# Five small moves in an attention and feed-forward kernel on one core: a bank for the ones, a load in halves, and squares, stores and a scale at later steps

## The chip, the cores and the metric

The kernel runs on one core of one Trainium2 chip. The metric is the device time of one execution in microseconds. Before the change the median of 3 runs is 811.76 us (811.22 to 811.85).

A core has five engines, each of which works through its own row of instructions in order: TensorE (PE, matrix products), VectorE (DVE), ScalarE (ACT), GpSimd (POOL) and SyncE (SP), which here issues nearly all DMA transfers. Engines wait for each other by semaphores.

## The reference

`x` is 2048 x 512 in float32. It is normalised, goes through windowed attention with 32 heads of 16 and, beside that, through a gated feed-forward net with 1792 inner columns. The result is `x + s * g`.

```python
xn = _layernorm(x, axis=-1)
# s: attention; idx = arange(S), W = 256, Dh = 16, H = 32
qkv = (xn @ wqkv) ...                       # q, k, v per head
scores = einsum("bhqd,bhkd->bhqk", q, k) * (Dh ** -0.5)
mask = (idx[:, None] - idx[None, :] >= 0) & (idx[:, None] - idx[None, :] < W)
p = softmax(where(mask, scores, -1e9))
s = (p @ v) @ wo
# g: feed-forward
h = silu(xn @ w1) * (xn @ w3)
g = silu(h @ w2)
return x + s * g
```

## The kernel before, in words

Tokens are worked on in four tiles `t` of 512 (`NT`), each of four blocks `b` of 128. Heads are in four groups `g` of eight, and a group's heads in two passes `p`. The 1792 inner columns are 14 blocks `f` of 128.

A float32 operand of a product is cut into two float16 numbers, hi and lo, and a product is three matmuls: hi·hi, lo·hi, hi·lo. Before a weight matrix is cut, the squares of its entries are summed per row (on ACT by `activation` with `accum_out`, L249, or on DVE, L251), the sums are cast (L261) and added over all rows by matmuls with a matrix of ones (`powers`, L280 or, in a corner of a bank of scores, L285); a short chain on DVE (L291 to L304) makes a power of two of them, with which ACT cuts the hi part (L333, or L342 and L343) and DVE (L334) or POOL (L345) the lo part.

PSUM, where PE writes, has three kinds of banks: two for plain products that take turns (`m0`, `m1`, by `bank()`), two for scores (`s`, by `scores_bank()`) and one for sums of attention (`po`). PE cannot write a bank before it has been read.

The order on PE is that of the program. The order on the other engines is made by the scheduler when the kernel is built. The program itself holds a clock of steps: `later(n, f)` puts `f` into a list that is due `n` steps on, and a step passes with each batch of scores and each piece of dense work. `beside_scores(n, f)` does the same for norms by matmuls in a corner of the scores' banks.

At the start PE is fed with ones (`keep_busy`), the first tile is normalised and transposed (`turn`, L493, with XH copied by ACT at L496 and XL made by DVE at L501), and groups 0 and 1 of queries and keys are projected (`project`, L597; evacuated by ACT at L614 and DVE at L618). Projected queries and keys are stored to DRAM (`dQ`, `dK`) and fetched in another layout by `fetch`. Then `spread` mixes batches of scores (maxima: PE L665, DVE L679; probabilities: PE L746, DVE L753, ACT L756; values: PE L774) with dense work (gate and up: PE L1036, ACT L1051, DVE L1055 and L1060; down: PE L1261; output: PE L1313).

For the first tile, the gate and up weights of two blocks are loaded (L868), and `measure(f)` sums their squares, one block per step when `apart` is 1, and lets the norm follow by `beside_scores(8, scale)`. `measure(6)` is called five steps late. The down weights' squares are L923. `wout` does the same for the output weights in units 6 and 7. `total` makes an output block; its store to DRAM (L1324) is due four steps after it, and its buffers (`slot`, from a pool of 54 that all blocks share) come free with the store.

Of the kernel before, what the change touches and what calls it, by code (L numbers as in the profile page):

```python
# [10 lines left out]
F32 = mybir.dt.float32  # L11
# [72 lines left out]
def tile_block(ctx: ExitStack, tc: tile.TileContext, x, wqkv, wo, w1, w3, w2, out):  # L84
# [59 lines left out]
    def later(n, f):  # L144
        made_so_far[0] += 1
        queue.append((now[0] + n, made_so_far[0], f))
# [16 lines left out]
    def bank(shape, dtype=F32):  # L163

        open_bank[0] = b = 1 - open_bank[0]
        return psm.tile(shape, dtype, name=f"m{b}", tag=f"m{b}", bufs=1)
# [15 lines left out]
    def beside_scores(n, f):  # L182

        later(n, lambda: besides.insert(0, f))
# [396 lines left out]
    def project(t, g, k, terms=(range(3),), scores_bank=False):  # L581


        cell = {}

        parts = ([[(c, i) for c in (2 * half, 2 * half + 1) for i in range(3)] for half in range(2)] if len(terms) == 1
                 else [[(c, i) for i in group for c in range(NC)] for group in terms])

        def part(n):
            assert turned[t] == 4  # L590
            w = WQ[t, g, k]
            xh, xl = X[t]
            if n == 0:
                cell["pp"] = pss.tile([P, 2, TW], F32, name="s")[:, 0, :] if scores_bank else bank([P, TW])
            for c, i in parts[n]:
                a, b = ((0, xh), (1, xh), (0, xl))[i]
                nc.tensor.matmul(cell["pp"], w[:, (a * NC + c) * P:(a * NC + c + 1) * P], b[:, c, :], start=(c, i) == parts[0][0],  # L597
                                 stop=(c, i) == parts[-1][-1])
            if n < len(parts) - 1:
                return  # L600
            if t == 0:
                def store():
                    with behind_load():
                        nc.sync.dma_start(dWQ[g, k], w)
                    give(w, after=8)
                later(45, store)
            else:
                give(w)
            pp = cell["pp"]
            both = take(F16)  # L610
            B = both.rearrange("p (a t) -> p a t", a=2)
            s = QS / (XS * WS)
            with urgent():
                nc.scalar.activation(B[:, 0, :], pp, AF.Copy, scale=s)  # L614

            def rest():
                with urgent():
                    lasts["emptied"] = nc.vector.scalar_tensor_tensor(B[:, 1, :], pp, s, B[:, 0, :], op0=ALU.mult, op1=ALU.subtract)  # L618
                d = (dQ, dK)[k][g][:, :, t * TW:(t + 1) * TW]
                if k == 0:  # L620
                    nc.sync.dma_start(d[:, 0:2, :], B[:, 0:1, :].to_broadcast([P, 2, TW]))
                    nc.sync.dma_start(d[:, 2, :], B[:, 1, :])
                else:
                    nc.sync.dma_start(d[:, 0:2, :], B)
                    nc.sync.dma_start(d[:, 2, :], B[:, 0, :])
                give(both, after=4)
            later(1, rest)
        return opening([(len(l), lambda n=n: part(n)) for n, l in enumerate(parts)])
# [2 lines left out]
        WQ[t, g, k] = w = take(F16)  # L631
        nc.sync.dma_start(w, dWQ[g, k])

    def fetch(t, g):
        QA[t, g] = qa = qpool.tile([P, 4, TW], F16, name="qa")
        ka = keys(t, g)
        c0 = 0 if t else 2 * P
        for dst, d in ((ka[:, :, c0:], dK[g][:, :, t * TW - 2 * P + c0:(t + 1) * TW]),
                       (qa, dQ[g][:, :, t * TW:(t + 1) * TW])):
            for r in range(2):  # L640
                lasts["load"] = nc.sync.dma_start(dst[64 * r:64 * r + KR],
                                  d[64 * r:64 * r + 64].rearrange("(a d) i t -> (d i) a t", d=DH))

# [224 lines left out]

    measured = set()

    def measure(f, apart=0):

        raws = [RAW.pop(f + i) for i in range(2)]
        sb = squares([raws[0][0], raws[1][0], raws[0][1], raws[1][1]], on_act=4 if f > 2 else 2, apart=apart)

        def scale(s=None):
            pp = small.tile([P, 2, 2], F32, name="pp")
            pi = small.tile([P, 2, 2], F32, name="pi")  # L880
            return then(s, powers(sb, 4, pp.rearrange("p a b -> p (a b)"), pi.rearrange("p a b -> p (a b)"), s),
                        lambda: rest(pp, pi))

        def rest(pp, pi):
            ff = slice(f, f + 2)
            nc.vector.tensor_scalar(sg_scale[:, ff], pp[:, 0, :], 0.5 / (WS * XS), None, op0=ALU.mult)
            nc.vector.tensor_mul(p13[:, ff], pp[:, 0, :], pp[:, 1, :])
            measured.update((f, f + 1))

            def cut(i, k):  # L890
                if k == 0:
                    WF[0, f + i] = [[None, None], WF.pop((0, f + i), [None, None])[1]]
                WF[0, f + i][0][k] = a = take(F16)
                split_pool(a[:, 0:D], a[:, D:], raws[i][k], pi[:, k, i:i + 1])
                give(raws[i][k], after=5)
            for i in range(2):
                for k in range(2):
                    later(((1, 2, 4, 6) if f < 8 else (1, 5, 9, 13))[2 * i + k], lambda i=i, k=k: cut(i, k))
        if started:
            beside_scores(8, scale)  # L900
        else:
            later(10 if apart else 6, scale)

# [389 lines left out]
    def total(t, b):  # L1293

        r = slice(t * TW + b * P, t * TW + (b + 1) * P)
        cell = {}

        def part(half):
            WOH, WOL = SQ["wo"][:2]
            tb = slice(b * P, (b + 1) * P)  # L1300
            if half == 0:
                cell["ps"] = bank([P, D])
                assert (t, b) in summed
                cell["y"] = y = take(F32)
                acc = ACC[t, b]
                with behind_exp():
                    nc.scalar.activation(y, acc, AF.Tanh, scale=0.5)
                nc.vector.scalar_tensor_tensor(y, y, 1.0, acc, op0=ALU.add, op1=ALU.mult)
                give(acc)
            ps, y = cell["ps"], cell["y"]  # L1310
            for g in (2 * half, 2 * half + 1):
                for i, (a, w) in enumerate(((0, WOH), (0, WOL), (1, WOH))):
                    nc.tensor.matmul(ps, O[t, g][:, a, tb], w[g], start=g == 0 and i == 0,  # L1313
                                     stop=g == NG - 1 and i == 2)
            if half:
                with urgent():
                    lasts["emptied"] = nc.vector.scalar_tensor_tensor(y, ps, sc["y"], y, op0=ALU.mult, op1=ALU.mult)
                if t == NT - 1:
                    nc.vector.tensor_add(y, y, XR[t, b])
                else:  # L1320
                    halves(nc.gpsimd.tensor_add, y, y, XR[t, b])

                def store():
                    nc.sync.dma_start(out[r, :], y)  # L1324
                    give(y, XR[t, b], after=30)
                if t == NT - 1:
                    store()
                else:
                    later(4, store)
                if b == 3:  # L1330
                    give(*(OT[t, g] for g in range(NG)))
        return opening([(6, lambda h=h: part(h)) for h in range(2)])
# [22 lines left out]
    def feed_forward():  # L1355
# [4 lines left out]
        for t in range(NT):  # L1360
            for f in range(FB):
                if t == 0:
# [3 lines left out]
                    elif f + LEAD == FB - 1:  # L1366
                        pieces += [(0, lambda f=f: load(0, f)) for f in range(FB - 2, FB)]
                    if f % 2 and f + 3 < FB:
                        pieces.append((0, lambda f=f + 3: later(5, lambda: measure(f, 1)) if f == 6 else measure(f, 1)))
                    pieces += [(0, lambda f=f: load_down(0, f)) for f in range(f + 2 if f else 0, min(f + 3, FB))]  # L1370
                    for m in range(f + 1 if f else 0, min(f + 2, FB)):
                        k = next(k for k, (_, f1) in enumerate(GROUPS) if m < f1)
# [158 lines left out]
        nc.gpsimd.memset(KA[2][:, a, :].bitcast(F32), TWO_ONES)  # L1531


    def keep_busy(n):
        ps = bank([P, 4, P])
        for _ in range(n):
            nc.tensor.matmul(ps, onesb, onesb.unsqueeze(1).to_broadcast([P, 4, P]), start=True, stop=True)

# [19 lines left out]
        flush()  # L1558
    with tc.issue_after(lasts["hi"].ins), tc.issue_after(lasts["x"].ins):
        qk[1][1]()  # L1560
    keep_busy(4)


    k00, q00 = (project(0, 0, k, ((0,), (1,), (2,)), k) for k in (1, 0))
    run([k00[0], q00[0], k00[1]])
    qk[1][2]()
    with tc.issue_after(lasts["scale"].ins):
# [2 lines left out]
    qk[1][3]()  # L1570
    with tc.issue_after(lasts["hi"].ins):
        run([k00[2], q00[2]])
    later(1, lambda: fetch(0, 0))
    k01 = project(0, 1, 1, ((0, 2), (1,)))
    run(k01[:1])
    wv[2]()
# [4 lines left out]
    sc["o"] = scaled(SQ["wv"][3], OS / WS, "so")  # L1581
    with tc.issue_after(lasts["hi"].ins):
        measure(0)
    run(project(0, 1, 0, scores_bank=True))
    later(1, lambda: fetch(0, 1))
    run(value(0, True))
    qk[2][1]()
# [35 lines left out]
    for n, u in enumerate(units):  # L1623
# [7 lines left out]
            wout[0]()  # L1631
        if n == 7:
            wout[1](2)
            beside_scores(12, lambda s: then(s, wout[2](s), lambda: later(2, lambda: wout[3](2)), lambda: later(3, out_scale)))
        want += a_unit - other[n]
        mine = more(want)

# [39 lines left out]
```

## Time and profile before

| | |
|---|---|
| median of 3 runs | 811.76 us |
| the profiled execution | 811.24 us |
| its span on the core | 809.4 us |
| PE busy | 793.7 us (98%) |
| DVE busy | 631.2 us (78%) |
| ACT busy | 392.1 us (48%) |
| POOL busy | 377.1 us (47%) |
| granted TensorE clock | 1.00 throughout |

Times in rows of the trace are in microseconds from the start of the span: first the start, then how long, then the engine and the line of the kernel, the operation, what is written from what and how large it is. In brackets stands how long the engine stood idle before the row and what ended it. "SPq" is SP's queue: how long the issue of a DMA took, not its transfer.

### The profile page before, as it was taken

Reading aid. Unit: us, or ns where it says so; the run is one execution under the profiler, and the core shown is the slowest. Engines: PE = TensorE matmul, PEld = TensorE weight load, DVE = VectorE, ACT = ScalarE, POOL = GpSimd, SP = SyncE. Lnnn points to the kernel's source line nnn. Section 1 sums busy time; section 2 is a strip of 40 time slices with the busy share of each in tenths; the row PEclk is TensorE's granted clock in tenths of the full one; section 3 lists DMA queues with packets and bytes.
Section 4 is the critical chain, followed back from the end, with each engine's and each line's share of the span. In section 5 each row is a group of like instructions: output and inputs, shape, how many; then the busy total and the mean of one; then the engine's idle time right before and its main releaser. Section 6 shows DMA issues by size and latency. Waiting matters only on the chain.

```text
span 809.4 us, 23944 instructions
## 1 busy us (share of the span) xinstructions
PE 793.7 (98%) x9176; PEld 403.7 (50%) x9176; DVE 631.2 (78%) x2037; ACT 392.1 (48%) x591; POOL 377.1 (47%) x732
## 2 busy tenths in 40 slices
PE   8999989999999999999999999999999999999998
PEld 4444444444444444444444454456544754466465
DVE  8788788887888777887988888777778787875437
ACT  6879586553546544345344433344444234344411
POOL 2345376342329445354353455530346276550670
PEclk9999999999999999999999999999999999999999
DMA  9968554835576474757655634646372644335321
GB/s 282 265 214 267 160 183 134 278 114 191 160 199 208 134 232 139 218 142 263 160 162 181 194 104 119 185 137 179 105 201 74 160 139 137 113 90 172 111 65 62
DMA packets 109795, 134.19 MB, mean 166 GB/s; under 512 B 18864, under 2 KB 64880, under 8 KB 109680
## 3 DMA queue, kind: packets, MB, share of 16 engines
q1 hardware_dynamic: 109392, 132.13, 54.6%
q8 instruction: 72, 1.18, 0.6%
q10 hardware_dynamic: 288, 0.52, 0.2%
q14 instruction: 43, 0.35, 0.1%
HBM read 91.23 MB, written 36.57 MB: 158 GB/s over the span
## 4 chain that ended last, share of the span: by engine, by line
PE 79%; DVE 8%; ACT 6%; DMA 3%; issue 2%; SPq 1%; POOL 0%; ACTq 0%; DVEq 0%
PE m L1036 30%; PE po L774 8%; PE m L1261 8%; PE m L1179 8%; PE m L597 7%; PE s L746 5%; PE m L1313 4%; PE m L567 4%; PE s L665 3%; DMA slot<-in_B_w_dram 2%; DVE junk L679 2%; PE po L665 2%; ACT slot L342 1%; ACT pt L756 1%; ACT sqa L249 1%
## 5 line engine op out<-in xcount | busy, mean ns | idle before, releaser
L1036 PE MATMUL m<-XH,slot 128*128 128x512 f16 x896 | 267.4, 380 | 1.6 <-DVE slot L618 1.2
L756 ACT ACTIVATE pt<-s,es 128x1024 f32<-128x1024 f32 x152 | 167.5, 1112 | 193.7 <-DVE s L753 186.5
L1036 PEld LDWEIGHTS <-slot 128*128 128x128 f16 x1344 | 124.7, 98 | 156.0 <-issue 12.0
L1036 PE MATMUL m<-XL,slot 128*128 128x512 f16 x448 | 169.9, 379 | 0.0
L753 DVE TENSOR_TENSOR s<-s,MK 128x256 f32<-128x256 f32 (+2 forms) x280 | 118.7, 434 | 51.2 <-PE s L746 47.0
L679 DVE CUSTOM_DVE_ANT_0 junk<-s,MW 128x320 bf16<-128x320 f32 x276 | 133.9, 485 | 17.9 <-PE s L665 10.3
L339 POOL TENSOR_TENSOR slot<-slot,slot 128x256 f16<-128x256 f32 (+1 forms) x86 | 57.7, 692 | 141.9 <-ACT slot L1069 76.7
L345 POOL TENSOR_TENSOR slot<-slot,slot 128x128 f16<-128x128 f32 x168 | 69.1, 446 | 58.3 <-ACT slot L343 58.3
L679 DVE CUSTOM_DVE_ANT_0 junk<-po,MW 128x320 bf16<-128x320 f32 x172 | 83.4, 485 | 4.7 <-DVE mt L704 0.3
L1261 PE MATMUL m<-slot,slot 128*128 128x512 f16 x336 | 78.6, 380 | 0.3 <-DVE slot L1055 0.3
L774 PE MATMUL po<-pt,V 64*32 64x320 f32 (+4 forms) x2880 | 77.2, 342 | 0.8 <-DVE pp L304 0.8
L597 PE MATMUL m<-XH,slot 128*128 128x512 f16 x240 | 71.0, 380 | 1.6 <-DVE slot L1055 1.2
L1179 PE MATMUL m<-slot,slot 128*128 128x256 f16 x588 | 68.4, 273 | 0.0
L1094 POOL TENSOR_TENSOR slot<-slot,slot 128x256 f16<-128x256 f32 x98 | 64.6, 671 | 1.1
L1051 ACT ACTIVATE slot<-m,sgs 128x512 f32<-128x512 f32 x56 | 38.3, 683 | 54.4 <-PE m L1036 52.3
L774 PEld LDWEIGHTS po<-pt,V 64*32 64x32 f32 x2880 | 50.5, 106 | 22.9 <-PE s L515 0.9
L1179 PEld LDWEIGHTS <-slot 128*128 128x128 f16 x588 | 56.1, 98 | 11.5 <-issue 3.0
L1055 DVE SCALAR_TENSOR_TENSOR slot<-slot,m 128x512 f32<-128x512 f32 x56 | 38.3, 684 | 29.0 <-ACT slot L1051 29.0
L746 PE MATMUL s<-qa,KA 50*64 50x320 f16 (+3 forms) x1472 | 58.4, 260 | 0.1
L597 PEld LDWEIGHTS <-slot 128*128 128x128 f16 x384 | 35.6, 98 | 44.8 <-issue 3.4
L746 PEld LDWEIGHTS <-KA 50*64 50x64 f16 x1472 | 30.1, 106 | 51.9 <-issue 30.9
L1261 PEld LDWEIGHTS <-slot 128*128 128x128 f16 x336 | 30.7, 98 | 38.6 <-issue 4.2
(189 smaller groups left out, 1138.5 us busy)
## 6 DMA issues: line engine op xcount, KB each, us to landing
slot<-dW SPq DMA_DIRECT2D x98, 256.0 KB
slot<-in_B_w_dram SPq DMA_DIRECT2D x56, 256.0 KB
slot<-dFold SPq DMA_DIRECT2D x48, 256.0 KB
dW<-slot SPq DMA_DIRECT2D x42, 256.0 KB
slot<-in_A_x_dram SPq DMA_DIRECT2D x30, 256.0 KB
KA<-dK SPq DMA_DIRECT2D x24, 288.0 KB
qa<-dQ SPq DMA_DIRECT2D x32, 192.0 KB
slot<-dWQ SPq DMA_DIRECT2D x24, 256.0 KB
```

The lines of the kernel that those rows point to most:

```text
L339: op(out[:, c], a[:, c], b[:, c])
L345: nc.gpsimd.tensor_sub(lo[:, c:c + P], raw[:, c:c + P], hi[:, c:c + P])
L597: nc.tensor.matmul(cell["pp"], w[:, (a * NC + c) * P:(a * NC + c + 1) * P], b[:, c, :], start=(c, i) == parts[0][0], stop=(c, i) == parts[ ...
L679: lasts["maximum"] = nc.vector.tensor_tensor_reduce(out=junk[:, :n], in0=s[:, r, :n], in1=mask, scale=1.0, scalar=NEG, op0=ALU.add, op1=AL ...
L746: nc.tensor.matmul(s[64 * h:64 * h + 64, r, o:o + 64 * n], ka[rows, 2 * p + a, 64 * (m + 4):64 * (m + 5)], qa[rows, 2 * p + a, 64 * (m + k ...
L753: nc.vector.tensor_add(v, v, MK[:, kind, of:of + n, :].unsqueeze(1).to_broadcast([P, 2 * len(which), n, 64]))
L756: lasts["exp"] = nc.scalar.activation(pt, s, AF.Exp, scale=es)
L774: nc.tensor.matmul(cell["po"][32 * i:32 * i + 32, h, 64 * (m + k):64 * (m + k + n)], V[64 * h:64 * h + 64, (4 * t + m // 2) % VB, hd * VW: ...
L1036: nc.tensor.matmul(cell[k], w[:, (a * NC + c) * P:(a * NC + c + 1) * P], b[:, c, :], start=c == 0 and i == 0, stop=c == NC - 1 and i == 2)
L1094: nc.gpsimd.tensor_sub(lo, view, hi)
L1179: nc.tensor.matmul(cell["ps"][:, c], made[:, f:f + P], wj[:, g:g + 256], start=j == j0 and c == 0 and n == 0, stop=j == j1 - 1 and n == 2, ...
L1261: nc.tensor.matmul(ps, hh[:, a * TW + b * P:a * TW + (b + 1) * P], w[:, c * D:(c + 1) * D], start=f == f0 and i == 0, stop=f == f1 - 1 and ...
```

## The change

It has five parts.

1. The ones that fill PE ahead of the first projection are three matmuls instead of four. They are written to the scores' bank into which the projection of keys then goes (`waiting`), not to a plain bank. The plain banks `m0` and `m1` change places from there on.
2. The first fetch, of tile 0 and group 0, is made for heads 0 and 1 first and then for heads 2 and 3: eight loads of half the size instead of four.
3. The squares of blocks 6 and 7 start eight steps late instead of five, and their norm is due six steps after that instead of eight.
4. The store of an output block of tiles 0 to 2 is due ten steps after it instead of four.
5. The norm of the output weights is due after fourteen steps instead of twelve.

```diff
@@ project
             if n == 0:
-                cell["pp"] = pss.tile([P, 2, TW], F32, name="s")[:, 0, :] if scores_bank else bank([P, TW])
+                cell["pp"] = bank([P, TW]) if scores_bank is False else scores_bank()[:, 0, :]
@@
-    def fetch(t, g):
+    def fetch(t, g, ps=None):
         QA[t, g] = qa = qpool.tile([P, 4, TW], F16, name="qa")
         ka = keys(t, g)
         c0 = 0 if t else 2 * P
-        for dst, d in ((ka[:, :, c0:], dK[g][:, :, t * TW - 2 * P + c0:(t + 1) * TW]),
-                       (qa, dQ[g][:, :, t * TW:(t + 1) * TW])):
-            for r in range(2):
-                lasts["load"] = nc.sync.dma_start(dst[64 * r:64 * r + KR],
-                                  d[64 * r:64 * r + 64].rearrange("(a d) i t -> (d i) a t", d=DH))
+        for heads in (slice(0, 4),) if ps is None else [slice(2 * p, 2 * p + 2) for p in ps]:
+            for dst, d in ((ka[:, heads, c0:], dK[g][:, :, t * TW - 2 * P + c0:(t + 1) * TW]),
+                           (qa[:, heads, :], dQ[g][:, :, t * TW:(t + 1) * TW])):
+                for r in range(2):
+                    rows = slice(64 * r + DH * heads.start, 64 * r + DH * heads.stop)
+                    lasts["load"] = nc.sync.dma_start(dst[64 * r:64 * r + KR],
+                                      d[rows].rearrange("(a d) i t -> (d i) a t", d=DH))
@@
-    def measure(f, apart=0):
+    def measure(f, apart=0, until=8):
...
-            beside_scores(8, scale)
+            beside_scores(until, scale)
@@ total
-                    later(4, store)
+                    later(10, store)
@@ feed_forward
-                        pieces.append((0, lambda f=f + 3: later(5, lambda: measure(f, 1)) if f == 6 else measure(f, 1)))
+                        pieces.append((0, lambda f=f + 3: later(8, lambda: measure(f, 1, 6)) if f == 6 else measure(f, 1)))
@@
-    def keep_busy(n):
-        ps = bank([P, 4, P])
+    def keep_busy(n, ps=None):
+        ps = bank([P, 4, P]) if ps is None else ps
@@
-    keep_busy(4)
+    waiting = scores_bank()
+    keep_busy(3, waiting[:, 0, :].rearrange("p (k q) -> p k q", q=P))
...
-    k00, q00 = (project(0, 0, k, ((0,), (1,), (2,)), k) for k in (1, 0))
+    k00, q00 = (project(0, 0, k, ((0,), (1,), (2,)), (lambda: waiting) if k else False) for k in (1, 0))
...
-    later(1, lambda: fetch(0, 0))
+    later(1, lambda: fetch(0, 0, (0, 1)))
...
-    run(project(0, 1, 0, scores_bank=True))
+    run(project(0, 1, 0, scores_bank=scores_bank))
@@
-            beside_scores(12, lambda s: then(s, wout[2](s), lambda: later(2, lambda: wout[3](2)), lambda: later(3, out_scale)))
+            beside_scores(14, lambda s: then(s, wout[2](s), lambda: later(2, lambda: wout[3](2)), lambda: later(3, out_scale)))
```

On PE the order of instructions changes in two places only: one ones matmul is gone, and the norm of the output weights stands behind a transpose of a later tile's block instead of ahead of it. On the other engines the scheduler orders anew. Three places follow, each before and then after; line numbers behind the first edits are two or three higher after.

SP at the first fetches. `slot_551` and `slot_552` before, `slot_553` and `slot_554` after, are the two halves of the query and key weights of group 3; `KA` and `qa` are where a fetch lands. Before:

```order
L622 DMA dQ_143<-slot_417 128x512
L395 DMA slot_551<-in_A_wqkv_dram 128x4x128
L625 DMA dK_148<-slot_462 128x512
L641 DMA KA_140<-dK_147 48x4x512 x2
L641 DMA qa<-dQ_143 48x4x512 x2
L624 DMA dK_148<-slot_462 128x2x512
L621 DMA dQ_144<-slot_495 128x2x512
L622 DMA dQ_144<-slot_495 128x512
L395 DMA slot_552<-in_A_wqkv_dram 128x4x128
L641 DMA KA_141<-dK_148 48x4x512 x2
L641 DMA qa<-dQ_144 48x4x512 x2
```

After:

```order
L622 DMA dQ_143<-slot_415 128x512
L625 DMA dK_148<-slot_464 128x512
L643 DMA KA_140<-dK_147 48x2x512 x2
L643 DMA qa<-dQ_143 48x2x512 x2
L643 DMA KA_140<-dK_147 48x2x512 x2
L643 DMA qa<-dQ_143 48x2x512 x2
L624 DMA dK_148<-slot_464 128x2x512
L621 DMA dQ_144<-slot_497 128x2x512
L622 DMA dQ_144<-slot_497 128x512
L395 DMA slot_553<-in_A_wqkv_dram 128x4x128
L643 DMA KA_141<-dK_148 48x4x512 x2
L643 DMA qa<-dQ_144 48x4x512 x2
```

The loads of heads 0 and 1 come first, the stores of group 1 behind all eight loads, and the two weight loads behind them; the second one (`slot_554`) follows the last row shown.

DVE at the norms of groups 2 and 3 of the query and key weights. `sb<-ssq 128x2` is the cast of group 3's sums of squares; `al`, `sw` belong to group 2's scale. Before:

```order
L294 TENSOR_SCALAR al<-s 128x1
L261 CAST sb<-ssq 128x2
L679 ISA junk,M<-s,MW 128x320
L679 ISA M 128x1
L295 SCALAR_TENSOR_TENSOR al<-s,al 128x1
```

After, from the same first row on, with the rows between left out here as they are the same as before but for the cast, and then the place to which it went:

```order
L294 TENSOR_SCALAR al<-s 128x1
L681 ISA junk,M<-s,MW 128x320
L681 ISA M 128x1
L295 SCALAR_TENSOR_TENSOR al<-s,al 128x1
L681 ISA junk,M<-s,MW 128x320
```

```order
L334 SCALAR_TENSOR_TENSOR slot_726<-slot_205,sw_643,slot_726 128x512
L1057 SCALAR_TENSOR_TENSOR slot_737<-slot_737,m_716 128x512
L681 ISA junk,M<-s,MW 128x320
L681 ISA M 128x1
L261 CAST sb<-ssq 128x2
```

The cast stands 18 rows later, behind group 2's scale and lo parts and behind the first product of the gate (L1055 before, L1057 after).

ACT at the evacuations of group 2's projections (L614) and the cut of group 3's weights (L333). L249 here are squares of blocks 4 and 5, L342 and L343 cut blocks 2 and 3. Before:

```order
L614 ACTIVATE slot_906<-m_884 128x512
L249 ACTIVATE sqa,ssq<-slot_701 128x512
L342 ACTIVATE slot_213<-slot_213,pi 128x512
L249 ACTIVATE sqa,ssq<-slot_705 128x512
L343 CAST slot_891<-slot_213 128x512
L342 ACTIVATE slot_214<-slot_214,pi 128x512
L614 ACTIVATE slot_972<-m_911 128x512
L343 CAST slot_918<-slot_214 128x512
L333 ACTIVATE slot_995<-slot_552,sw_932 128x512
L333 ACTIVATE slot_998<-slot_551,sw_932 128x512
```

After:

```order
L614 ACTIVATE slot_908<-m_886 128x512
L343 CAST slot_835<-slot_210 128x512
L925 ACTIVATE sqa,ssq_739<-slot_714 128x512
L342 ACTIVATE slot_213<-slot_213,pi 128x512
L249 ACTIVATE sqa,ssq<-slot_703 128x512
L343 CAST slot_893<-slot_213 128x512
L614 ACTIVATE slot_974<-m_913 128x512
L249 ACTIVATE sqa,ssq<-slot_707 128x512
L342 ACTIVATE slot_214<-slot_214,pi 128x512
L333 ACTIVATE slot_997<-slot_554,sw_934 128x512
L343 CAST slot_920<-slot_214 128x512
L333 ACTIVATE slot_1000<-slot_553,sw_934 128x512
```

Two rows that stood ahead of the second L614, a square and a cut, now stand behind it, ahead of the first L333. Of the squares of blocks 6 and 7, the first stood ahead of the third L333 of the down weights further on and the second ahead of the fourth; all four now stand behind the fourth.

## Prediction

> **What bounds the kernel now.** I read the page first, then the busy time by stretches, then each row on which TensorE (PE) waited.
>
> ```profile
> span 809.4 us, 23944 instructions
> PE 793.7 (98%) x9176; PEld 403.7 (50%) x9176; DVE 631.2 (78%) x2037; ACT 392.1 (48%) x591; POOL 377.1 (47%) x732
> ...
> 0.00:30.00 30.00, 27.17 (x129) 12.61 (x129) 23.63 (x74) 21.88 (x42) 5.33 (x33) 1.00 0.96 277
> 30.00:61.00 31.00, 29.75 (x209) 12.86 (x209) 25.41 (x117) 24.13 (x53) 16.94 (x36) 1.00 0.81 231
> 61.00:80.00 19.00, 17.70 (x142) 7.88 (x142) 16.12 (x60) 18.90 (x37) 10.86 (x22) 1.00 0.83 268
> ...
> 110.00:135.00 25.00, 20.73 (x296) 10.62 (x295) 21.80 (x80) 20.42 (x38) 16.48 (x38) 1.00 0.41 123
> ...
> 200.00:740.00 540.00, 539.54 (x6716) 275.98 (x6715) 430.17 (x1349) 234.61 (x307) 257.96 (x452) 1.00 0.54 159
> ```
>
> The columns of a stretch are its length, then PE, weight loads, DVE, ACT and POOL busy, the granted clock, the DMA share and GB/s. PE is the bound: 793.7 of 809.4 us, at clock 1.00. What a change can win is PE's idle time, and that lies early: 2.83 us up to 30, 1.25 up to 61, 1.30 up to 80, 4.27 between 110 and 135. From 200 to 740 it is 0.46 in all. Three of the five edits act up to 80; PE waits there in the first four of these rows (the last column is the idle time and what ended it):
>
> ```profile
> 12.85 1.02 PE L1537 MATMUL m<-onesb 128*128 128x512 bf16 x4 [0.58 <-DVE XL L501]
> 30.15 0.30 PE L665 MATMUL s<-KA,qa 48*64 48x128 f16 x7 [0.41 <-DMA qa<-dQ]
> 55.33 0.59 PE L1036 MATMUL m<-XH,slot 128*128 128x512 f16 x2 [1.03 <-DVE slot L618]
> 76.93 0.33 PE L665 MATMUL po<-KA,qa 48*64 48x320 f16 x4 [0.84 <-DVE M L679]
> ...
> 115.04 0.59 PE L597 MATMUL m<-XH,slot 128*128 128x512 f16 x2 [1.19 <-DVE slot L1055]
> 118.47 0.30 PE L665 MATMUL s<-KA,qa 48*64 48x256 f16 x4 [1.62 <-ACT pt L756]
> ```
>
> **Part 1, the ones.** Three ones matmuls instead of four, into a bank that nobody is reading, so the 0.58 for DVE and one matmul (1.02 us for four, some 0.22 apart) leave PE's row. What comes late next:
>
> ```profile
> 12.41 0.62 ACT L496 CAST XH<-s 128x512 f16<-128x512 f32 x1
> 13.71 1.03 PE L597 MATMUL s<-XH,slot 128*128 128x512 f16 x4
> 15.67 0.16 DVE L261 CAST sb<-ssq 128x2 bf16<-128x2 f32 x1
> 16.30 0.19 PE L280 MATMUL s<-sb,onesb 128*128 128x1 bf16 x2
> ```
>
> The projection needs the last XH copy, which ends at 13.03, so it starts near 13.08 and not 13.71. Three groups of four (0.86 each, from the spacing of the same rows) bring PE to the weight norms at 15.66. Those need DVE's cast, which ends at 15.83 and does not move, since DVE's work there hangs on ACT and not on these matmuls. PE goes on at 15.89 instead of 16.30: 0.41 us. Bounds: 0, if the chain behind the norms does not follow, and 0.80, the wait and the matmul whole. I take 0.41.
>
> **Part 2, the first loads in halves.** SyncE (SP) issues the loads and stores in order:
>
> ```profile
> 22.49 0.43 SPq L395 DMA_DIRECT2D slot<-in_A_wqkv_dram  x1
> 23.01 0.50 SPq L625 DMA_DIRECT2D dK<-slot  x1
> 24.48 0.82 SPq L641 DMA_DIRECT2D KA<-dK  x2
> 25.39 0.88 SPq L641 DMA_DIRECT2D qa<-dQ  x2
> 26.32 0.44 SPq L624 DMA_DIRECT2D dK<-slot  x1
> ...
> 27.88 0.82 SPq L395 DMA_DIRECT2D slot<-in_A_wqkv_dram  x1
> ...
> 31.88 0.80 SPq L641 DMA_DIRECT2D qa<-dQ  x2
> ```
>
> The first scores need only heads 0 and 1, now the first four of eight loads. Half of 768 KB is no longer ahead of them, nor the 256 KB weight load at 22.49, which moves behind. At the 277 GB/s of the first stretch that is (384 + 256) / 277 = 2.3 us sooner, so PE, arriving 0.41 earlier, finds its queries there and the 0.41 at 30.15 goes. Bounds 0 to 0.41; I take 0.41, since 2.3 us covers it several times. The price is on SP: four more issues of 0.44 delay the stores of group 1 by 1.8 us, and the second half of group 3's query and key weights (slot_552 before, slot_554 now) is issued behind the next four loads, at about 32.68 + 1.8 = 34.4 instead of 27.88. The qa loads took 30.15 - 26.27 = 3.9 us from the end of issue until PE went on, so this half lands near 38.3, and its square ends near 39.1.
>
> **What the new order does between 37 and 55.** The scheduler has moved the cast that waits for that square:
>
> ```profile
> 37.47 0.17 DVE L261 CAST sb<-ssq 128x2 bf16<-128x2 f32 x1 [1.60 <-ACT sqa L249]
> 39.47 1.34 ACT L333 ACTIVATE slot<-slot,sw 128x512 f16<-128x512 f32 x2 [1.45 <-DVE sw L302]
> 41.56 0.68 DVE L1055 SCALAR_TENSOR_TENSOR slot<-slot,m 128x512 f32<-128x512 f32 x1
> 42.29 0.59 PE L1036 MATMUL m<-XH,slot 128*128 128x512 f16 x2
> 44.99 0.62 ACT L1069 CAST slot<-slot 128x512 f16<-128x512 f32 x1 [2.25 <-DVE slot L1060]
> 50.20 0.58 ACT L614 ACTIVATE slot<-m 128x512 f16<-128x512 f32 x1
> ...
> 53.65 0.58 ACT L614 ACTIVATE slot<-m 128x512 f16<-128x512 f32 x1
> ```
>
> Before, DVE stood 1.60 us at 37.47; behind it lay the scale for which ACT stood 1.45, and behind that the product (L1055) that frees the bank for the matmuls at 42.29, some 0.2 late. Now the cast stands behind the product. ACT ran dry at 39.47 - 1.45 = 38.02; it comes 0.41 earlier and has one square (0.7) less ahead, so the weights' cut starts near 37.1, 2.3 us earlier. The 0.2 goes. ACT's cast at 44.99 follows DVE and comes 2.2 earlier, and both evacuations L614, with one cut fewer ahead of the second, about 2.1: 48.1 and 51.5.
>
> DVE's L618 behind the second then ends near 53.1. PE, 0.41 + 0.41 + 0.2 = 1.0 ahead, comes at 54.30 - 1.0 = 53.3, so the 1.03 at 55.33 goes too. Bounds 0 to 1.03, by how far ACT really gains; I take 1.0, as 53.1 lies on the near side. PE's lead is 2.0.
>
> **What is given back between 55 and 77.** ACT now has a square and a cut ahead of the two L333, and DVE puts L1060 between the two L334:
>
> ```profile
> 57.72 0.48 DVE L679 CUSTOM_DVE_ANT_0 junk<-s,MW 128x320 bf16<-128x320 f32 x1
> ...
> 60.98 1.34 ACT L342 ACTIVATE slot<-slot,pi 128x512 f32<-128x512 f32 x2 [1.64 <-DVE pi L302]
> ...
> 72.18 0.69 ACT L1051 ACTIVATE slot<-m,sgs 128x512 f32<-128x512 f32 x1
> 72.96 0.67 DVE L1055 SCALAR_TENSOR_TENSOR slot<-slot,m 128x512 f32<-128x512 f32 x1
> ```
>
> L1060 needs PE's f=1 block, done 1.5 us of matmuls after PE resumes at 53.3, so near 55.0; L1060 and L334 (0.65 each) put the maxima (L679) at 56.3 instead of 57.72. That is 1.4 earlier, as is ACT's L342 at 60.98. From there ACT works without a pause (18.90 of 19.00 us), and through 72.18 and 72.96 its backlog sets when DVE frees the bank at 76.93. So PE's 2.0 shrinks to 1.4: minus 0.6. Bounds: 0 and minus 2.0.
>
> **Part 3, squares of blocks 6 and 7.** They and their cast stand later. Up to L1051 at 72.18 ACT's row holds the same kinds as often, with one square of the down weights (L923) in place of one of these, each of one 128x512 block; the third and fourth L333 stand one place earlier. The product at 72.96 waits for L1051, not for them, so I cost this at 0; at best it takes the 0.84 at 76.93. PE's own order of the norms does not change, and the cast reaches DVE while ACT has little to do after 80 (19.48 busy of 30 in the stretch below), so nothing is lost.
>
> ```profile
> 80.00:110.00 30.00, 29.80 (x349) 14.35 (x348) 23.91 (x94) 19.48 (x37) 12.76 (x36) 1.00 0.64 198
> ```
>
> **Parts 4 and 5, stores and output weights.** SP stands for the stores:
>
> ```profile
> SPq L1324 <- POOL slot L339: 22.6, 10, 4.4
> ```
>
> 22.6 us of SP's time in ten waits, behind which weight loads queue. Six steps later most should be ready when SP comes. But it lies behind 200, where PE lost 0.46 in 540 us: the cover is PE's matmuls, and stores and scale together can win at most 0.46. Slots come free six steps later, which could make a load wait; with SP freed of waits I take 0, ends minus 0.46 and plus 0.5, as much again the other way. The waits at 115.04 and 118.47 stay: ACT, DVE and POOL keep their order there, and after ACT's slack behind 80 all engines move with PE.
>
> **Sum.** 0.41 + 0.41 + 0.2 + 1.0 - 0.6 = 1.42 us. The profiled execution took 811.24 us (span 809.4 and 1.8 around it), 0.5 under the median; it would take 809.8. From the median, 811.76 - 1.42 = 810.3.
>
> **Rivals.** *All given back:* ACT's backlog from 61 to 77 does not move although PE does, say because the weights that it cuts land no sooner; DMA at 0.83 of its time there speaks for it, the 1.64 that ACT waits at 60.98 for DVE against. Then 0 to 0.6 remain: 811.5.
>
> *Nothing given back, and the squares help:* ACT and DVE keep PE's 2.0, and the earlier L333 take some of the 0.84: 811.76 - 2.0 - 0.5 = 809.3. For it speaks that DVE stood for L618 and L1055 at each of these waits; against, that the work ahead of L1051 is the same.
>
> *The late weight half decides (slower):* DVE now stands at its cast behind L1055, near 40.5. A landing at 38.3 leaves 1.4 us there. Behind it lie four maxima and L1060, needed by PE near 44.5 where they would be done at 42.1, so 2.4 more. From a landing at about 42 on, each microsecond costs PE one, and it also takes the 2.0 won at 55. A landing at 44 costs 2 and leaves the 0.8 of parts 1 and 2: 811.76 - 0.8 + 2 = 813.0. For it: the DMA engines are 0.96 busy and SP's eight loads queue; against: the 3.9 us measured for the same kind of load.
>
> The row for the loads says 0.44 us of SP each. The Trainium skill ("DMA: Bandwidth & Descriptors", Rules for kernel authors) says to coalesce small transfers, and its section on the anatomy of one DMA gives a fixed cost of about 2.0 us for each. Were that paid in line, four more loads would put the half 8 us and not 1.8 us later, an estimate from that page, and this rival would hold. The rows 24.48 to 26.32 show issues 0.44 apart, so the trace speaks against paying it in line.
>
> **Chances.** Below 0.2% (1.6 us, about what a measurement of this kernel can tell from no change) I call it the same. Forecast 0.42, its own range 809.7 to 811.0, of which 0.19 lies beyond 1.6 us; nothing given back 0.28; all given back 0.13; late weight half 0.17. Faster 0.19 + 0.28 = 0.47, same 0.23 + 0.13 = 0.36, slower 0.17. The range 808.8 to 812.4 takes in the second rival with 0.5 below it and the milder half of the slower one.
>
> **What would show it.** Right: no DVE wait before the projection, which starts near 13.1; no wait for qa near 29.5; DVE's 1.60 at its cast gone; PE's wait at 55.33 under 0.3; the waits near 76 larger than before; those at 115 and 118 as long as now. Wrong: the cast behind L1055 waiting more than 1 us; PE's lead at 61 under 1; or new PE waits between 200 and 740 for slots.

## The result, and the profile after

The changed kernel takes 814.52 us (median of 6 runs, 813.82 to 815.20) against 811.47 for the kernel before (6 runs, 811.10 to 811.85): 1.0037 times as long, with an interval of 1.0024 to 1.0050. It is 3.05 us slower. 810.3 was forecast, within 808.8 to 812.4: wrong in sign, and outside the range. The profiled execution took 815.2 us.

The head of the page of the changed kernel:

```profile
span 813.4 us, 23978 instructions
...
PE 795.1 (98%) x9175; PEld 404.8 (50%) x9175; DVE 635.8 (78%) x2037; ACT 391.6 (48%) x591; POOL 377.9 (46%) x732
```

Its busy time by stretches, with the columns of the prediction (length, PE, weight loads, DVE, ACT, POOL, granted clock, DMA share, GB/s):

```profile
0.00:30.00 30.00, 27.15 (x140) 12.54 (x141) 23.75 (x76) 22.07 (x42) 5.33 (x33) 1.00 0.90 259
30.00:61.00 31.00, 30.38 (x224) 13.41 (x222) 26.30 (x124) 25.45 (x55) 17.17 (x36) 1.00 0.90 258
61.00:80.00 19.00, 17.82 (x128) 7.84 (x127) 15.57 (x55) 17.39 (x35) 10.96 (x22) 1.00 0.71 242
110.00:135.00 25.00, 20.93 (x297) 10.78 (x296) 21.74 (x80) 20.68 (x38) 16.50 (x39) 1.00 0.49 138
200.00:740.00 540.00, 536.29 (x6663) 273.19 (x6662) 432.06 (x1341) 231.69 (x305) 258.34 (x452) 1.00 0.55 158
...
256.00:270.00 14.00, 11.04 (x164) 5.34 (x162) 13.28 (x33) 5.96 (x9) 11.13 (x20) 0.88 0.41 104
```

Between 200 and 740, where PE had stood idle for 0.46 us before, it now stands idle for 3.71, and 2.96 of that lies in the 14 us from 256 to 270. The clock there is 0.88. Before, the same stretch read:

```profile
256.00:270.00 14.00, 13.99 (x211) 6.65 (x204) 12.79 (x40) 6.92 (x11) 11.82 (x21) 1.00 0.37 107
```

How far ahead PE is can be read from the same batch of values in both kernels, at three places. Before, then after:

```profile
82.74 0.50 PE L774 MATMUL po<-pt,V 64*32 64x320 f32 x8
...
352.43 0.40 PE L774 MATMUL po<-pt,V 64*32 64x256 f32 x8
...
752.25 0.44 PE L774 MATMUL po<-pt,V 64*32 64x256 f32 x7
```

```profile
81.13 0.50 PE L776 MATMUL po<-pt,V 64*32 64x320 f32 x8
...
355.85 0.40 PE L776 MATMUL po<-pt,V 64*32 64x256 f32 x8
...
755.97 0.43 PE L776 MATMUL po<-pt,V 64*32 64x256 f32 x5
```

PE is 1.61 us ahead at 82, 3.42 behind at 352 and 3.72 behind at 752. The batch that starts at 264.30 before starts at 267.70 after, already 3.40 behind. So the early edits win 1.6 us, and 5.0 us are lost in one place, between 256 and 268.

The early part, PE's rows of the changed kernel that answer to those shown of before:

```profile
13.30 0.38 PE L597 MATMUL s<-XH,slot 128*128 128x512 f16 x1 [0.16 <-ACT XH L496]
16.10 0.20 PE L280 MATMUL s<-sb,onesb 128*128 128x1 bf16 x2
29.66 0.25 PE L667 MATMUL s<-KA,qa 48*64 48x128 f16 x4
53.84 0.38 PE L1038 MATMUL m<-XH,slot 128*128 128x512 f16 x1 [0.62 <-DVE slot L618]
75.32 0.33 PE L667 MATMUL po<-KA,qa 48*64 48x320 f16 x4 [0.70 <-DVE M L681]
113.41 0.38 PE L597 MATMUL m<-XH,slot 128*128 128x512 f16 x1 [0.83 <-DVE slot L1057]
116.84 0.30 PE L667 MATMUL s<-KA,qa 48*64 48x256 f16 x4 [1.63 <-ACT pt L758]
```

The waits for XL and for `qa` are gone, that at 55.33 has shrunk from 1.03 to 0.62 us, and those at 115 (0.83 instead of 1.19) and 118 are still there. PE goes on 1.5 to 1.6 us earlier behind each of the last four.

Now the place of the loss. PE, then ACT, DVE and POOL of the changed kernel in time order:

```profile
258.76 0.42 PE L748 MATMUL s<-qa,KA 50*64 50x320 f16 x12 [1.47 <-ACT pt L758]
259.65 0.42 PE L748 MATMUL s<-qa,KA 50*64 50x320 f16 x12 [0.47 <-DVE XL L525]
...
261.27 1.06 PE L1038 MATMUL m<-XH,slot 128*128 128x512 f16 x2
...
264.95 0.59 PE L1038 MATMUL m<-XH,slot 128*128 128x512 f16 x2 [0.17 <-DVE slot L1057]
...
267.57 0.33 PE L667 MATMUL s<-KA,qa 48*32 48x320 f16 x8 [0.74 <-ACT pt L758]
```

```profile
248.01 1.33 ACT L342 ACTIVATE slot<-slot,swwo 128x512 f32<-128x512 f32 x2 [0.83 <-DVE swwo L302]
...
255.86 0.58 ACT L614 ACTIVATE slot<-m 128x512 f16<-128x512 f32 x1
257.60 1.11 ACT L758 ACTIVATE pt<-s,es 128x1024 f32<-128x1024 f32 x1 [1.16 <-DVE s L755]
...
256.48 0.69 DVE L618 SCALAR_TENSOR_TENSOR slot<-m,slot 128x512 f16<-128x512 f32 x1 [1.90 <-ACT slot L614]
...
259.92 4.05 DVE L824 TENSOR_SCALAR dr<-dr,so 128x32 f32<-128x32 f32 x1
263.89 0.42 DVE L755 TENSOR_TENSOR s<-s,MK 128x256 f32<-128x256 f32 x1
...
250.50 6.21 POOL L345 TENSOR_TENSOR slot<-slot,slot 128x128 f16<-128x128 f32 x16 [3.27 <-ACT slot L343]
...
263.54 0.40 POOL L1008 CAST slot<-slot 128x256 f16<-128x256 f32 x1
264.02 1.30 POOL L1009 TENSOR_TENSOR slot<-slot,slot 128x256 f16<-128x256 f32 x2
```

Two things meet. First, the later scale puts the output weights' cuts (L342 and L343) on ACT from 248.01 on. Before, the first of them ran at 241.23 and the last was done by 247. They now stand just ahead of the evacuation L614, for which DVE stands 1.90 us at L618; the mask L755, the exponential L758 and PE's scores follow it late: 1.47 + 0.47 us. Second, DVE's product of `dr` with `so`, 32 columns and 0.24 us where nothing holds it, takes 4.05 us. It ends at 263.97, when POOL, busy without a gap from 250.50, pauses for 0.08 us ahead of 264.02. All that stands behind it on DVE comes 3.8 us later than without the hold. Before, POOL's stretch ran from 255.72 to 262.33 and the same product in it took 0.52.

### The profile page after: what moved, and what is told of

Read it like the earlier page. It is cut to its first block, busy times and chain, and to the rows that moved or that the text cites. A ratio compares the mean times of both kernels' runs of the same rounds, so it can differ in the third digit from the quotient of the medians.

```text
span 813.4 us, 23978 instructions
## 1 busy us (share of the span) xinstructions
PE 795.1 (98%) x9175; PEld 404.8 (50%) x9175; DVE 635.8 (78%) x2037; ACT 391.6 (48%) x591; POOL 377.9 (46%) x732
## 5 line engine op out<-in xcount | busy, mean ns | idle before, releaser
L1038 PE MATMUL m<-XH,slot 128*128 128x512 f16 x896 | 268.5, 381 | 1.5 <-DVE slot L618 0.8
L758 ACT ACTIVATE pt<-s,es 128x1024 f32<-128x1024 f32 x152 | 167.6, 1112 | 197.2 <-DVE s L755 192.2
L1038 PEld LDWEIGHTS <-slot 128*128 128x128 f16 x1344 | 125.4, 98 | 156.8 <-issue 14.4
L1038 PE MATMUL m<-XL,slot 128*128 128x512 f16 x448 | 170.5, 381 | 0.0
L755 DVE TENSOR_TENSOR s<-s,MK 128x256 f32<-128x256 f32 (+2 forms) x280 | 118.7, 434 | 50.4 <-PE s L748 47.2
L345 POOL TENSOR_TENSOR slot<-slot,slot 128x128 f16<-128x128 f32 x168 | 69.4, 448 | 62.9 <-ACT slot L343 62.9
L1057 DVE SCALAR_TENSOR_TENSOR slot<-slot,m 128x512 f32<-128x512 f32 x56 | 38.3, 685 | 28.8 <-ACT slot L1053 28.8
## 6 DMA issues: line engine op xcount, KB each, us to landing
slot<-dW SPq DMA_DIRECT2D x98, 256.0 KB
slot<-in_B_w_dram SPq DMA_DIRECT2D x56, 256.0 KB
slot<-dFold SPq DMA_DIRECT2D x48, 256.0 KB
dW<-slot SPq DMA_DIRECT2D x42, 256.0 KB
slot<-in_A_x_dram SPq DMA_DIRECT2D x30, 256.0 KB
slot<-dWQ SPq DMA_DIRECT2D x24, 256.0 KB
```

What stands on the lines that cost most here:

```text
L345: nc.gpsimd.tensor_sub(lo[:, c:c + P], raw[:, c:c + P], hi[:, c:c + P])
L755: nc.vector.tensor_add(v, v, MK[:, kind, of:of + n, :].unsqueeze(1).to_broadcast([P, 2 * len(which), n, 64]))
L758: lasts["exp"] = nc.scalar.activation(pt, s, AF.Exp, scale=es)
L1038: nc.tensor.matmul(cell[k], w[:, (a * NC + c) * P:(a * NC + c + 1) * P], b[:, c, :], start=c == 0 and i == 0, stop=c == NC - 1 and i == 2)
```

## The experiments

**Which part costs.** Four kernels: part 5 alone on the kernel before, and the changed kernel without 5, without 4 and 5, and with parts 1 and 2 alone. They share one group of runs of the kernel before (811.43).

```diff
@@ only5: the kernel before with
-            beside_scores(12, lambda s: then(s, wout[2](s), ...
+            beside_scores(14, lambda s: then(s, wout[2](s), ...
@@ no5: the changed kernel with
-            beside_scores(14, lambda s: then(s, wout[2](s), ...
+            beside_scores(12, lambda s: then(s, wout[2](s), ...
@@ no45: and with
-                    later(10, store)
+                    later(4, store)
@@ p12: and with
-  ... later(8, lambda: measure(f, 1, 6)) if f == 6 else measure(f, 1)))
+  ... later(5, lambda: measure(f, 1)) if f == 6 else measure(f, 1)))
```

> The kernel before with part 5 alone: the norm of the output weights due after 14 steps. Theory A: PE waits for ACT near 260.3 as in the changed kernel, and matmuls go at half speed for 2 to 4 us; slower than before by 3 to 6 us, 814.5 to 817. Theory B: no such wait, within 1 us of before.

> The changed kernel with the norm of the output weights due after 12 steps again, as before; parts 1 to 4 stay. Theory A (part 5 alone costs: the cuts of the output weights now fall on ACT just ahead of an evacuation, PE waits 1.5 us at 258.8 and runs at half speed after): PE's early lead of 1.65 us at 165 stays to the end, no PE wait over 0.3 us near 257, ratio to before 0.997 to 0.999, some 809.5 to 810.3. Theory B (part 4's stores or the early lead itself, by another phase between ACT and PE, make the wait near 258.8): the wait stays, 813 to 815.

> Parts 1 to 3 alone: stores due after 4 steps and output weights after 12, as before. If part 4 costs or wins nothing, the time is that of parts 1 to 4 within 0.3 us. If the stores wait less for a cause that the trace of before hid, it is 0.5 us or more slower than parts 1 to 4.

> Parts 1 and 2 alone. If part 3 (squares of blocks 6 and 7) is worth nothing, as the prediction has it, the time is that of parts 1 to 3 within 0.3 us, and PE's lead at 115 is 1.6 us as in the changed kernel. If part 3 won some of the waits near 73 to 77, it is 0.4 to 0.8 us slower than parts 1 to 3.

| kernel | median, us | against before |
|---|---|---|
| part 5 alone | 816.67 | 1.0068 (1.0055 to 1.0081) |
| parts 1 to 4 | 810.72 | 1.0012 (0.9989 to 1.0036) |
| parts 1 to 3 | 810.99 | 1.0004 (0.9989 to 1.0020) |
| parts 1 and 2 | 811.07 | 1.0006 (0.9985 to 1.0026) |

Part 5 alone costs 5.2 us and explains more than the whole loss. The other medians lie 0.4 to 0.7 us under before, but of 35 executions of these three kernels five took 817 to 821 us, which is why the intervals, which go by all executions, reach over 1. The kernel before can take as long, if seldom: one of its 21 executions in the next group of runs took 819.19 us, and none of 57 in the others. So parts 3 and 4 together are worth no more than 0.35 us, if anything.

Parts 1 to 4 were expected at 809.5 to 810.3 us and took 810.72. The wait near 258.8 is gone, as theory A has it, but PE's early lead does not stay whole. It is 1.7 us at 197 and 1.45 at 264, as PE, being early, waits for DVE's cast ahead of the norm of the output weights:

```profile
236.30 0.28 PE L285 MATMUL s<-sb,onesb 64*64 64x1 bf16 x12 [0.29 <-DVE sb L261]
```

In the profiled execution of part 5 alone PE's clock stays whole, although a stretch at half speed had been expected, and the loss shows as plain waits:

```profile
260.21 0.42 PE L746 MATMUL s<-qa,KA 50*64 50x320 f16 x12 [1.59 <-ACT pt L756]
261.10 0.42 PE L746 MATMUL s<-qa,KA 50*64 50x320 f16 x12 [0.47 <-DVE XL L525]
266.40 0.59 PE L1036 MATMUL m<-XH,slot 128*128 128x512 f16 x2 [1.87 <-DVE slot L1055]
269.02 0.33 PE L665 MATMUL s<-KA,qa 48*32 48x320 f16 x8 [0.74 <-ACT pt L756]
```

1.59 + 0.47 lie behind the evacuation, 1.87 + 0.74 behind the held product: 4.67 us in all.

The profiled execution of parts 1 to 3 was one of the long ones (818.87 us). It shows the same hold at another instruction, the negated maxima, which take 0.17 us where nothing holds them:

```profile
245.89 7.78 DVE L693 TENSOR_SCALAR NM<-M 128x16 f16<-128x16 f32 x1
...
252.35 1.28 POOL L339 TENSOR_TENSOR slot<-slot,slot 128x256 f16<-128x256 f32 x2
...
255.47 0.64 PE L748 MATMUL s<-qa,KA 50*64 50x320 f16 x8 [5.52 <-ACT pt L758]
```

DVE's instruction ends at 253.67 and POOL's last one at 253.63. PE waits 5.52 us for what follows.

**Is it the form of the product?** The product keeps its engine and place, and takes a tile of ones as a second input.

```diff
-                nc.vector.tensor_scalar(dr, dr, sc["o"], None, op0=ALU.mult)
+                nc.vector.scalar_tensor_tensor(dr, dr, sc["o"], onesb[:, 0:32], op0=ALU.mult, op1=ALU.mult)
```

> The changed kernel, with one instruction in another form: the product of dr with the scale so (DVE TENSOR_SCALAR, 4.05 us at 259.92 in the changed kernel, 0.24 where nothing holds it) is made by SCALAR_TENSOR_TENSOR with a tile of ones as second input; value, place and engine are the same. Theory A2 (part 5 costs in two ways: the weights' cuts stand ahead of the evacuation on ACT, which makes PE wait 1.47 + 0.47 us, and the TENSOR_SCALAR then falls into a stretch where POOL runs without a gap, 250.5 to 263.94, and is held to its end, which costs PE the rest of the 5 us): the instruction takes under 0.8 us, the waits of 1.47 and 0.47 stay, the wait of 0.74 on L758 goes; 812.0 us if TensorE's granted clock stays whole, 813.6 if it falls to a half for 3.4 us as in the changed kernel. Rival R1 (the held instruction is only a companion, all of the loss comes from ACT's queue): 814.5. Rival R2 (the other form is held as long): the instruction again takes about 4 us, 814.5.

814.38 us, no better than the changed kernel. (The ratio to before is 1.0025, with a wide interval of 0.9986 to 1.0065, since the execution of 819.19 us is in this group of the kernel before, whose median is 811.23.) Rival R2 is right: the other form is held just as long.

```profile
259.74 4.09 DVE L824 SCALAR_TENSOR_TENSOR dr<-dr,so,onesb 128x32 f32<-128x32 f32 x1
```

So this run takes no hold away and leaves theory A2 untested.

**The hold taken away.** The product moves to ACT, which stands idle there, in the changed kernel and in the kernel with part 5 alone.

```diff
-                nc.vector.tensor_scalar(dr, dr, sc["o"], None, op0=ALU.mult)
+                nc.scalar.activation(dr, dr, AF.Copy, scale=sc["o"])
```

> The changed kernel, with the product of dr with so (the DVE instruction that was held 4.05 us behind POOL, and as long with a second input in SBUF) made on ACT, which stands idle from 259.6 to 265.3 there. Theory A2: no DVE instruction is held at 260, so DVE's L755 comes 3.5 us sooner; the waits of 1.47 and 0.47 us on L748 stay, since ACT's queue ahead of the evacuation is unchanged; the waits of 0.17 and 0.74 after it go; 812.0 us if the granted clock stays whole, 813.6 if it falls to a half for 3.4 us behind the two waits. Rival R1 (the held instruction costs nothing of its own, ACT's queue is the whole loss): 814.4. Rival R6 (the next DVE instruction that shares with POOL is held in its place): one of over 2 us there, 814 or more.

> The kernel before with part 5 alone (816.67 us; PE waits of 1.59, 0.47, 1.87 and 0.74 us at 260 to 269, the granted clock whole) and the product of dr with so on ACT. Theory A2: 1.59 + 0.47 = 2.06 us of ACT's queue stay, 1.87 + 0.74 = 2.6 go, so 816.67 - 2.6 = 814.1 us, or up to 1.7 more if the clock falls to a half for 3.4 us. Rival R1 (ACT's queue is the whole loss): 816.7. Rival R7 (the hold was the whole loss): 811.5.

The changed kernel goes from 814.52 to 813.13 us (1.0020, 1.0011 to 1.0029), in two groups: five executions of ten at 811.66 to 812.55, five at 813.71 to 814.82. Part 5 alone goes from 816.67 to 814.17 us (1.0039, 1.0026 to 1.0052), where 814.1 was expected. PE's first two waits stay and the later ones are gone, in the changed kernel with the product on ACT:

```profile
258.66 0.42 PE L748 MATMUL s<-qa,KA 50*64 50x320 f16 x12 [1.49 <-ACT pt L758]
259.55 0.42 PE L748 MATMUL s<-qa,KA 50*64 50x320 f16 x12 [0.47 <-DVE XL L525]
```

So the hold costs 2.5 us of the 5.2 of part 5 alone, and the rest stays, most of it in the two waits behind the evacuation (1.40 and 0.47 us in that profile). The two groups fit the two cases of the expectation, with the clock whole (812.0) and at a half for 3.4 us (813.6): the mean granted clock is 0.999 to 1.000 in the first and 0.995 to 0.998 in the second.

**The scale later still.** At 20 in place of 14, the cuts stand behind the evacuation on ACT, and POOL's L345 come four at a time. The second kernel is the one before with that alone.

```diff
@@ w20: the changed kernel with
-            beside_scores(14, lambda s: then(s, wout[2](s), ...
+            beside_scores(20, lambda s: then(s, wout[2](s), ...
@@ only20: the kernel before with
-            beside_scores(12, lambda s: then(s, wout[2](s), ...
+            beside_scores(20, lambda s: then(s, wout[2](s), ...
```

> The changed kernel with the output weights' scale later still (20 in place of 14), so that on ACT the weights' cuts L342 and L343 stand behind the evacuation L614 and the exponentials L758 that follow it, no longer ahead of them, and POOL's differences L345 come after the products of the folds. Theory A2: no wait of PE over 0.3 us on L758 at 256 to 260, no DVE instruction of over 1 us there, and the time is that of the kernel without part 5, 810.7 us. Rival R3 (a later scale costs as such, since ACT, DVE and POOL have no room for its work after 248): 814 or more. Rival R4 (it meets the same hold at another place): one DVE TENSOR_SCALAR of 2 to 8 us there, 813 to 818.

> The kernel before with the output weights' scale at 20 in place of 12 and nothing else: on ACT the weights' cuts stand behind the evacuation L614 and its exponential, where the changed kernel has them ahead. Theory A2: nothing late at 256 to 270; 811.0 to 811.4 us, the time of before, or a few tenths less since the norm's wait of PE on sb (0.05 us at 237.75) moves. Rival R3 (a later scale costs as such): over 812. Rival R8 (the 809.4 us of the changed kernel with the scale at 20 comes from the scale at 20 and not from parts 1 and 2): 809.8 or less.

The changed kernel with the scale at 20 takes 809.40 us, 0.9982 of before (0.9972 to 0.9991), and beats both kernels. The kernel before with the scale at 20 takes 811.08 (0.9995, 0.9986 to 1.0004), the time of before. So neither R3 nor R8 holds: a later scale is no harm as such, and the gain of 1.7 us between the two is that of parts 1 to 4 (1.5 where each is taken against its own group of runs of the kernel before, 811.23 and 811.41). The first was expected at 810.7, the time without part 5; at 20 PE no longer waits for the norm's cast either, and the lead stays whole. With the scale at 20, ACT reaches the evacuation 2.3 us sooner than in the changed kernel, and PE doesn't wait. The rows of ACT and DVE in the changed kernel with the scale at 20, and the stretch from 256 to 270:

```profile
253.51 0.60 ACT L614 ACTIVATE slot<-m 128x512 f16<-128x512 f32 x1
...
256.23 0.29 DVE L824 TENSOR_SCALAR dr<-dr,so 128x32 f32<-128x32 f32 x1
```

```profile
256.00:270.00 14.00, 13.95 (x197) 6.86 (x196) 12.19 (x42) 11.26 (x18) 13.52 (x29) 1.00 0.47 114
```

This run moves ACT's and POOL's work at once; that the first two waits come from ACT's queue rests on it and on the two runs with the product on ACT, in which of the waits between 258 and 270 these two alone stay. No run moves ACT's cuts and leaves POOL's rows where they are.

**Both forms changed, without part 5.**

```diff
-                nc.vector.tensor_scalar(nm[:, 0, :], Mf, -1.0 / ONE, None, op0=ALU.mult)
+                nc.vector.scalar_tensor_tensor(nm[:, 0, :], Mf, -1.0 / ONE, onesb[:, 0:16], op0=ALU.mult, op1=ALU.mult)
```

> The changed kernel without part 5 (the scale at 12 as before), and with both small DVE TENSOR_SCALARs that were seen held behind POOL made by SCALAR_TENSOR_TENSOR with ones as second input: the product of dr with so (4.05 us in the changed kernel) and the negated maxima NM (7.78 us at 245.89 in the profiled execution of parts 1 to 3). Theory A2 (the executions of 817 to 819 us that parts 1 to 4 showed, 3 of 12, come from that hold alone): every execution between 809.5 and 812, median 810.6. Rival R2 (the form doesn't matter, any DVE instruction on that path is held): 1 to 4 of 12 executions at 816 to 820 as before. Rival R5 (the other form costs time of its own, 32 + 16 instructions): median 811.5 or more.

810.16 us (0.9983, 0.9974 to 0.9993; 0.9987 by the medians, as the execution of 819.19 us counts here too), all 11 executions between 809.77 and 810.55. That is what A2 expected, but the run with `dr` in the same form had shown that form to be held too. With three long executions of twelve in the kernel without this edit, none in eleven can be chance (0.75 to the 11th power is 0.04; with five of 35, 0.18). Whether the form helped stays open.

## Why the prediction was wrong

**The step that failed** is the term for parts 4 and 5, and in it part 5: "it lies behind 200, where PE lost 0.46 in 540 us: the cover is PE's matmuls, and stores and scale together can win at most 0.46", with plus 0.5 as the other end. The 0.46 bounds what can be won there and says nothing of what can be lost. The loss was sized by the gain, "as much again the other way". What it should have asked is who waits for the instructions that the moved work now stands ahead of: on ACT the evacuation L614, for which DVE's L618 waits, and for that PE's next scores. Part 5 alone costs 5.2 us where 0 was put down. About half of it, the waits behind the evacuation, lay in the order of ACT's rows. The other half, the 4 us hold of DVE's product, could not be read from the rows of before: the same product stood in a stretch of POOL there too, and took 0.52. The sixteen L345 push that stretch to later, and the runs do not show why the hold falls on the product there.

**Part 1, 0.41: right.** The norms' row is at 16.10 in the changed kernel, 0.20 earlier than before. But its first norm (L280) came at 9.11 and before's at 8.89, ahead of any edit; without these 0.22 the gain is 0.42.

**Part 2, 0.41: right but for 0.1.** The wait for `qa` is gone; one of 0.10 for DVE takes its place at 29.66. The late weight half (slower, 0.17) did not decide: SP issued the eight loads 0.46 us apart, from 24.55 to 28.20, the squares of the half were done at 39.91, and DVE's cast of it at 40.63 did not wait. (The 2.0 us that the prediction takes from the anatomy of one DMA stand in the Trainium skill under the heading of DMAs that GpSimd issues; here SP issues them.)

**The wait at 55.33, 1.0: mis-sized.** It shrank by 0.41 only. ACT's evacuation began at 51.70, close to the forecast 51.5, but DVE's L618, whose end had been put near 53.1, began only at 53.10 and let PE go at 53.84. It fits that the forecast kept the 0.36 us that lay between the evacuation's end and L618 before. They became 0.81, since two maxima stand ahead of L618 on DVE, the first of them behind a pause:

```profile
52.15 0.49 DVE L681 CUSTOM_DVE_ANT_0 junk<-po,MW 128x320 bf16<-128x320 f32 x1 [0.43 <-DVE al L298]
...
53.10 0.69 DVE L618 SCALAR_TENSOR_TENSOR slot<-m,slot 128x512 f16<-128x512 f32 x1
```

**Given back, minus 0.6: did not happen.** PE is 1.49 us ahead at 53.84, 1.61 at 75.32 and 1.63 at 113.41, and the wait near 76, which was to grow, went from 0.84 to 0.70. So two terms were off by 0.6 to 0.7 each, and their errors cancel: that the early sum of 1.42 measured 1.6 is in part luck. With the scale at 20 this lead shows in the time whole, 811.08 to 809.40.

**Part 3, 0: right as far as the runs tell** (810.99 against 811.07). **Part 4, 0: likewise** (810.72 against 810.99). But the two profiles with stores after four steps and the early lead show PE waits for a weight load, of which those with stores after ten have none: 0.29 and 0.21 us in parts 1 to 3, and this one in parts 1 and 2:

```profile
337.45 0.61 PE L597 MATMUL m<-XH,slot 128*128 128x512 f16 x2 [0.60 <-DMA slot<-dWQ]
```

So part 4 may win a few tenths that the medians cannot tell from chance.

None of the rivals was the mechanism. The line "or new PE waits between 200 and 740" named the sign of it, though for slots; no chance was given to it. The 0.17 on slower stood for the late weight half, which was not the cause.

## What to carry to other kernels

A stretch in which the bound engine never waits is no cover for moved work: its idle time caps the gain, not the loss. Price a move by the instruction that it now stands ahead of in each engine's row, and by who waits for that. Where POOL runs long stretches without a gap, look for short DVE instructions inside them on PE's path. Here moving one of them to ACT gave back 1.4 and 2.5 us, and a second input in SBUF gave back nothing.

## What the runs showed of the hardware

**A DVE instruction can be held far longer than one POOL instruction.** Over the nine profiled executions of the first two sets of runs, 229 of the `dr` and NM products began while POOL was at work. 23 took no longer than where nothing holds them. About 200 ended within 0.08 us behind the end of POOL's current instruction or the next one, at most 0.7 us late. Four were passed by at every boundary until POOL had a gap: 4.05, 4.06 and 4.09 us (eight POOL instructions) and 7.78 us (eighteen). The Trainium skill ("SBUF — State Buffer", Who interferes with whom) says that where DVE takes the port that it shares with POOL, the one of the two that issues first has it for the whole instruction and the other blocks. The usual case agrees; these four went on past the instruction that was running, and the measurement decides. That the two engines' shared port is what holds them is argued from that rule and from the matching ends, not shown. What decides at a boundary is open: in the profiles of parts 1 and 2 and of parts 1 to 3, NM begins 0.09 us into an L345; the one took 0.36 us, the other 7.78.

**The clock was halved behind two short waits.** The busy time by stretches of 1 us in the changed kernel:

```profile
259.00:260.00 1.00, 0.53 (x24) 0.31 (x16) 1.00 (x6) 0.60 (x2) 1.00 (x2) 1.00 0.00 0
260.00:261.00 1.00, 1.00 (x15) 0.47 (x8) 1.00 (x2) 0.00 (x0) 1.00 (x3) 0.84 0.00 0
261.00:262.00 1.00, 1.00 (x4) 0.29 (x2) 1.00 (x1) 0.00 (x0) 1.00 (x4) 0.50 0.00 0
...
263.00:264.00 1.00, 1.00 (x4) 0.42 (x3) 1.00 (x2) 0.00 (x0) 0.94 (x2) 0.50 0.00 0
264.00:265.00 1.00, 0.82 (x5) 0.25 (x3) 1.00 (x3) 0.00 (x0) 0.98 (x2) 0.96 0.10 16
```

After waits of 1.47 and 0.47 us with small matmuls between them, the granted clock is 0.50 for about 3.4 us, and L1038's matmuls come 0.43 us apart instead of 0.22. The Trainium skill ("TensorE: Matmul & The Clock Gate", What's actually happening) names an idle window of about 3.4 us as the cause; here PE was idle for 1.94 of the 3.41 us ahead of the half stretch, so a window that is idle in part can do. It doesn't always: part 5 alone has waits of 1.59 and 0.47 us at the same place, and its clock stays whole. In the traces' records of the clock, each stretch at half between the start and the end of a kernel lasts 3.41 us, and the stretch at full ahead of it a whole multiple of that (75 times, 256.0 us, in the changed kernel), so where the waits fall on such a grid may decide. Busy time alone does not: PE was busy for 0.43 of the step of the grid ahead of this half stretch, and steps of 0.42 (parts 1 to 3) and 0.45 (part 5 alone) left the clock whole.

In the changed kernel the 1.7 us so lost mostly fill the time in which PE would have waited for the held product: it waits 0.17 us for L1057, and 1.87 in part 5 alone. With the product on ACT they fit the difference between its two groups of executions.
